# Attention and a feed-forward layer in one kernel: another order of VectorE's sums, copies and scalings around two stages

## The chip, the cores and the metric

The kernel runs on one core of a Trainium2 chip. A core has TensorE (PE, the matrix engine), VectorE (DVE), ScalarE (ACT), GpSimd (POOL) and SyncE (SP, which here only starts transfers). Each engine works through its own instructions strictly in the order in which they were written; engines wait for one another only through semaphores. TensorE writes into eight PSUM banks, which VectorE and ScalarE empty. The metric is the device time of one execution in microseconds (us), taken as a median over runs.

## The reference

```python
def _attn_ref(q, k, v):                       # (8, 12, 448, 64) each
    scale = 1.0 / np.sqrt(q.shape[-1])
    scores = scale * np.matmul(q, k.transpose(0, 1, 3, 2))
    scores = scores - np.max(scores, axis=-1, keepdims=True)
    attn = np.exp(scores)
    attn = attn / (np.sum(attn, axis=-1, keepdims=True) + 1e-09)
    return np.matmul(attn, v).astype(np.float32)

def _moe_ref(x, w_in, w_out):                 # x (3584, 768), w_in (768, 2048), w_out (2048, 768)
    h = x @ w_in
    g = np.maximum(0.01 * h, h)
    return (g @ w_out).astype(np.float32)
```

The attention's output, with the heads side by side, is the `x` of the second function: 3584 tokens of 768 columns.

## The kernel before, in words

**Units of attention.** A unit is one pair of heads of one of the 8 batches; there are 48 units, 6 to a batch. For each unit TensorE computes scores in chunks (L337), ScalarE takes the exponential of each chunk (L351), and TensorE forms the weighted sums of v (`rows`: L877 for units below 18, L888 and L893 from unit 18 on). VectorE divides by the row sums: a reciprocal (L899) and a product (L900) that writes the tile `x` of the unit. The tile is then transposed into `xT`: for most units by a DMA started on SP (L294), and for units 9, 10, 11 and 17 (`X_PE`) by TensorE (L395) with a copy out of PSUM by VectorE (L396). Units of the second kind wait in the list `owed_x` until `settle_x` finds a score slot free. From unit 18 on keys are laid out so that a fourth, partial chunk of scores (the "rest", L356 and L358) belongs to each unit; it waits in `owed_rest`.

**PSUM.** Two banks g102 and g103 (`banks`) serve the feed-forward products, and three double slots sc104, sc105 and sc106 (`slots`) serve scores, weighted sums and the transpositions of L395, used in turn. A burst (`burst`) issues three chunks of scores, two matmuls each, into three slots.

**Stages of the feed-forward layer.** The tokens are cut into 7 stages. For stage i > 0, `hidden(i)` computes h = x·w_in with seven block products in place of eight (a Strassen-like scheme), so it needs sums of blocks of `w_in` (`mix_w_in`: 12 differences at L465 and then 4 sums at L469, each 128x768) and of the stage's own columns of `xT` (`mix_x_part`, eight differences at L494 written to `x_mix` and back into `xT`, four for the first two columns of blocks and four for the third). Then `second(i)` computes the output in two pairs of token blocks (`block_pair`, c = 0 and c = 1), again with seven products of eight matmuls each (L621) instead of eight. In a pair the products alternate between bank b and bank a. VectorE empties a bank by a copy (L626, `keep`) before the next product accumulates on it, or adds it to the output tile `o` (L629, `join`); and it forms two differences of h for the later products (L633 after the first product, L639 after the second). The third product needs the result of L633 and the bank b that L626 has emptied. In stage 0 `mix_first` adds to this, for pair c = 1, differences of `h` (L521, L522) inside pair c = 0. The finished `o` is stored by DMAs on SP (L408).

**The order of the work.** The order is written out when the program is built. `block_pair` yields at each step (a step is two matmuls, or the place behind a product's copies); x counts the steps of a pair: x = 1, 2, 3 lie inside the first product, and at x = 4 L633 and the first copy have been issued. At each step `second` calls `place`, which issues bursts, rests and weighted sums where a small model of time says that slot and data are ready. With `calm` false `place` issues neither rests nor weighted sums. After `place`, `second` advances the iterators: `ins` (the sums of `mix_w_in`), `outs` (those of `mix_weights`), `mix_first`, and `x_sums` (the two lists of L494 for the next stage; the second list waits for `owed_x` to be empty). Each of these adds instructions to VectorE's queue at that place.

Stage 1 needs the units of batch 2, 12 to 17, so the second list of its L494 needs unit 17, the one whose `x` goes through L395 and L396. Stage 6, the last, needs units up to 47, whose weighted sums are issued in stage 5.

Of the kernel before, what the change touches and what calls it, by code (L numbers as in the profile page):

```python
# [16 lines left out]
def kernel(  # L17
# [20 lines left out]
    NU = B * HP  # L38
# [6 lines left out]
    NR = len(cuts) - 1  # L45
    HEAD = S
    need = [HP * -(-t // S) for t in cuts]
# [24 lines left out]
    def next_slot():  # L72

        slots.append(slots.pop(0))
        return slots[-1]
# [230 lines left out]
    def transposes(u, bank=None):  # L306
        if u >= min(NPE, NU):
            return
        gone.add(u)
        for parts in ((1,), (0,)) if u == 0 else ((0, 1),):  # L310
            tr = turn_tile(bank)
            for i in parts:
                for so in range(NSC):
                    nc.tensor.transpose(  # L314
                        tr[:, i, ts(so, SC)], qk_sb[u][:SC, i * NSC + so], ident[:SC, :SC]
                    )
            if u == 0:
                stay_warm(3 if parts == (1,) else 5)
            at = slice(parts[0], parts[-1] + 1)
            (nc.scalar.copy if u == NPE - 1 or u == 0 and parts == (1,) else nc.vector.tensor_copy)(  # L320
                qkT[u % NQ][:, :QL].rearrange("p (i s) -> p i s", i=2)[:, at], tr[:, at]
            )
# [502 lines left out]
    owed_rest = []  # L825
    total = WIDE * NSC + (NU - WIDE) * NWC

    def at_chunk(x):

        return divmod(x, NSC) if x < WIDE * NSC else (WIDE + (x - WIDE * NSC) // NWC, (x - WIDE * NSC) % NWC)  # L830

    def scored():

        return owed_rest[0] if owed_rest else at_chunk(chunk)[0]

    def set_rest():

        u = owed_rest.pop(0)
        rest(u)
        return u  # L840
# [66 lines left out]
    def turned(u):  # L907

        return u < to["pe"] or to["pe"] == NPE and u < to["turn"]

    def burst(lazy=0):
        nonlocal chunk
        todo = [at_chunk(chunk + x) for x in range(3) if chunk + x < total]
        assert rows_done > todo[-1][0] - NE and turned(todo[-1][0]) and to["v"] > rows_done and not owed_rest
        if todo[0][0] >= WIDE:
            assert todo[0][1] == 0
            owed_rest.append(todo[0][0])
        for a, c in todo:
            scores(a, c)
        assert not late  # L920
        for a, c in todo[:3 - lazy]:
            expo(a, c)
        late.extend(todo[3 - lazy:])
        chunk += len(todo)

    X_PE = (HP + 3, HP + 4, HP + 5, 3 * HP - 1)
    owed_x = []

    def settle_x(now=None):
        while owed_x and (now is None or owed_x[0][1] <= now and model["free"].get(id(slots[0]), 0.0) <= now + 0.05):  # L930
            model["free"][id(slots[0])] = model["now"] + 1.0
            model["now"] += 0.3
            x_transposes(owed_x.pop(0)[0], next_slot()[:, 0])
# [39 lines left out]
    def place(i, want, soon=0, full=True, calm=True, first=False, lazy=0, keen=NU, cap=NU):  # L973

        free, ready = model["free"], model["ready"]
        done, state = 0, 0
        while True:
            settle_x(model["now"])
            now = model["now"]
            last = at_chunk(chunk + 2)[0]  # L980
            blocked = rows_done <= min(last, NU - 1) - NE
            u = rows_done
            whole = u < scored()
            at = [free.get(id(x), 0.0) for x in slots]
            u = to["pe"]
            if max(want, soon) > done and u <= min(last, NPE - 1) and len(slots) == 3 and at[0] <= now + 0.05:
                t = slots[0]
                transposes(u, next_slot()[:, 0])
                to["pe"] += 1
                model["now"] = now + 0.45  # L990
                free[id(t)] = model["now"] + 1.0
                continue
            if len(slots) < 3 and full and max(want, soon) > done and u <= min(last, NPE - 1) and state == 0:
                transposes(u)
                to["pe"] += 1
                state = 1
                model["now"] += 0.45
                continue
            if want > done and state < 2 and turned(last) and not blocked and not owed_rest and len(slots) == 3 and all(
                x <= now + 0.05 + 0.2 * j for j, x in enumerate(at)  # L1000
            ):
                state = 2
                order = list(slots)
                start = chunk
                burst(lazy)
                if first:
                    feed(start // 3)
                done += 1
                for x, t in enumerate(order[:chunk - start]):
                    model["act"] = max(model["act"], now + 0.45 + 0.2 * x) + 0.8  # L1010
                    free[id(t)] = model["act"] + (0.3, 0.15 + 0.5 * (lazy > 1), 0.15 + 0.5 * lazy)[x]
                    if at_chunk(start + x + 1)[1] == 0 and not owed_rest:
                        ready[at_chunk(start + x)[0]] = model["act"] + 0.1
                model["now"] = now + 0.78
                continue
            u = to["pe"]
            if first and full and state == 0 and u < min(NPE - 1, to["cast"] - 1) and u <= scored() + 1 and model["act"] <= now + 0.6:
                transposes(u)
                to["pe"] += 1
                state = 1  # L1020
                model["now"] += 0.45
                continue
            if calm and owed_rest and at[0] <= now + 0.05:
                t = slots[0]
                u = set_rest()
                model["act"] = max(model["act"], now + 0.25) + 0.5
                free[id(t)] = model["act"] + 0.15
                ready[u] = model["act"] + 0.1
                model["now"] = now + 0.19
                continue  # L1030
            u = rows_done
            if calm and whole and not (lazy and late) and at[0] <= now + 0.05 and ready.get(u, 0) <= now + 0.05 and (
                u <= at_chunk(chunk + 5)[0] - NE or u < keen
            ) and u < cap:
                t = slots[0]
                rows()
                if first:
                    pay()
                model["now"] = now + 1.08
                free[id(t)] = now + 2.33  # L1040
                continue
            return done

    def second(i):

        x_sums = [mix_x_part(i + 1, slice(0, 2)), mix_x_part(i + 1, slice(2, 3))] if i + 1 < NR else []
        fresh, summed = [None, None], [i + 1 == NR] * 2
        left = plan[i]
        for c in range(len(spots(i)[1])):
            for x, _ in enumerate(block_pair(i, c)):  # L1050
                if x % 4 == 0:
                    advance(i + 1 < NR and rows_done >= need[i + 2] - 3 and not all(summed), at_chunk(chunk + 3 * left - 1)[0])
                if c or x:
                    model["now"] += 0.325
                left -= place(i, left, calm=x not in (1, 2), keen=need[min(i + 2, NR)], cap=NU if all(summed) else need[i + 2])
                if i == 0 and c == 0 and x in (5, 7):
                    next(outs)
                if i == 0 and c == 0 and x in (9, 13, 17, 21):
                    mix_first((x - 9) // 2, 1, slice(HEAD - 3 * P, P))
                if i == 0 and c and x % 4 == 2:  # L1060
                    next(ins, None)
                for y in range(2):
                    if fresh[y] is None and i + 1 < NR and rows_done >= need[i + 2] - 1 + y:
                        fresh[y] = model["now"] + (2.5 if need[i + 2] - 2 + y in X_PE else 7.0)
                for y, todo in enumerate(x_sums if x % 2 == 0 else ()):
                    if fresh[y] is not None and fresh[y] <= model["now"] and not summed[y] and not (y and owed_x):
                        summed[y] = next(todo, 0) is not None
                        if not summed[y]:
                            break
        assert left == 0 or chunk == total, (i, left)  # L1070
        assert i + 1 == NR or rows_done >= need[i + 2], (i, rows_done)
        settle_x()
        for todo in x_sums:
            for _ in todo:
                pass
# [64 lines left out]
```

## Time and profile before

| what | value |
|---|---|
| median of 3 runs | 382.3 us (382.08 to 382.34) |
| profiled execution, its own time | 382.59 us |
| span of that execution, first to last instruction | 380.8 us |
| granted TensorE clock, mean | 0.999 |
| ScalarE, GpSimd busy | 253.2 us, 152.5 us |
| stage 0, pair c = 0 (first and last L621) | about 73 to 88.4 us |
| stage 0, pair c = 1 | about 89 to 104.5 us |
| first L549 of stage 1 and of stage 6 | 104.49 us, 339.92 us |

The page gives for each engine the busy time and its share of the span. The timeline gives instructions in order: start, time from the start to the end of the last one of the row, engine, line, operation, output and inputs, count, and in brackets how long the engine had been idle before and what released it. Instructions of one engine overlap a little: a row's own time can be longer than the distance to the start of the next, so in what follows distances between starts are used where an engine runs without a break. The chain of waits lists the pieces of the path that ended last in the same way.

### The profile page before, as it was taken

The numbers are of one execution on the slowest core, as the hardware profiler recorded it, in microseconds if no ns is written. First come the engines' busy times: TensorE is split into PE (matmuls) and PEld (weight loads), VectorE is DVE, ScalarE is ACT, GpSimd is POOL, SyncE is SP. The second block draws the span as 40 slices with busy tenths as digits, with TensorE's granted clock in tenths as the row PEclk, the third lists the DMA queues.
The fourth block names the chain that finished last, engine by engine and source line by source line (L and its number), as shares of the span: only waits on it lengthen the run. The fifth ranks groups of instructions, "written<-read, shape, count | busy, mean of one in ns | idle before, by whom it ended". The sixth has DMA issues, their size and how long they took to land.

```text
span 380.8 us, 9900 instructions
## 1 busy us (share of the span) xinstructions
PE 372.5 (98%) x3972; PEld 261.8 (69%) x3973; DVE 231.5 (61%) x513; ACT 253.2 (67%) x392; POOL 152.5 (40%) x302
## 2 busy tenths in 40 slices
PE   8999999999999999999999999999999999999995
PEld 6665658756498565896658965589755896668753
DVE  4662767786666555568475674655746565574753
ACT  5997885866667867677684776847867478318700
POOL 5886664495433854338333364334733000000000
PEclk9999999999999999999999999999999999999999
DMA  7999999999588996999858999579986540320022
GB/s 154 182 195 203 198 183 208 174 142 179 77 159 101 90 183 136 152 148 93 141 102 141 123 106 142 117 136 135 107 115 135 123 83 0 108 80 18 0 84 84
DMA packets 107198, 47.95 MB, mean 126 GB/s; under 512 B 79248, under 2 KB 103824, under 8 KB 107152
## 3 DMA queue, kind: packets, MB, share of 16 engines
q0 software_dynamic: 48096, 22.24, 48.7%
q1 hardware_dynamic: 58320, 24.43, 34.1%
q10 hardware_dynamic: 736, 0.66, 0.6%
q8 instruction: 31, 0.51, 0.5%
q14 instruction: 15, 0.12, 0.1%
HBM read 45.61 MB, written 11.01 MB: 149 GB/s over the span
## 4 chain that ended last, share of the span: by engine, by line
PE 94%; ACT 2%; DVE 2%; issue 1%; DVEq 0%
PE g L621 34%; PE sc L549 14%; PE g L549 14%; PE sc L337 9%; PE sc L888 6%; PE g L430 4%; PE sc L877 3%; PE g L716 2%; ACT e L351 2%; PE sc L893 2%; PE sc L356 1%; PE g L258 1%; PE g L314 1%; PE g L368 1%; PE sc L430 1%
## 5 line engine op out<-in xcount | busy, mean ns | idle before, releaser
L351 ACT ACTIVATE e<-sc 128x896 bf16<-128x896 f32 (+1 forms) x162 | 137.4, 922 | 42.4 <-PE sc L337 42.2
L621 PEld LDWEIGHTS <-h 128*128 128x128 bf16 x680 | 62.8, 98 | 50.2 <-issue 12.8
L621 PE MATMUL g<-w_out_sb,h 128*128 128x384 bf16 x448 | 86.5, 327 | 0.0
L538 ACT ACTIVATE h<-c 128x512 bf16<-128x512 f32 (+1 forms) x72 | 43.7, 611 | 28.6 <-DVE c L564 13.7
L549 PEld LDWEIGHTS <-w_in_sb 128*128 128x128 bf16 x576 | 54.7, 98 | 5.9
L337 PE MATMUL sc<-qkT 64*128 64x448 bf16 x324 | 42.8, 353 | 2.4 <-DVE xT L396 0.7
L626 DVE COPY o<-g 128x384 f32<-128x384 f32 x53 | 29.4, 555 | 24.3 <-PE g L621 24.2
L209 POOL COPY v<-fv 128x256 f32<-128x256 f32 (+1 forms) x38 | 15.2, 407 | 71.7 <-PE sc L893 47.5
L549 PEld LDWEIGHTS <-w_in_mix 128*128 128x128 bf16 x432 | 41.1, 98 | 4.0
L621 PE MATMUL g<-w_mix,h 128*128 128x384 bf16 (+1 forms) x224 | 41.9, 324 | 0.5 <-DVE o L626 0.5
L629 DVE TENSOR_TENSOR o<-o,g 128x384 f32<-128x384 f32 x42 | 23.2, 552 | 20.0 <-PE g L621 18.2
L888 PEld LDWEIGHTS <-e 128*128 128x128 bf16 x720 | 30.4, 97 | 3.5 <-ACT e L351 2.3
L888 PE MATMUL sc<-v,e 128*128 128x65 bf16 x720 | 32.1, 193 | 0.0
L209 POOL COPY qkb<-fq 112x256 f32<-112x256 f32 x38 | 16.6, 436 | 38.6 <-DMA fq<-in_q_dram 20.3
L337 PEld LDWEIGHTS <-qkT 64*128 64x128 bf16 x324 | 12.8, 94 | 25.6 <-issue 18.3
L900 DVE TENSOR_TENSOR x<-sc,rec 112x512 bf16<-112x512 f32 x42 | 29.0, 691 | 1.5
L899 DVE RECIPROCAL rec<-sc 112x8 f32<-112x8 f32 x42 | 8.7, 208 | 33.3 <-PE sc L893 17.2
L549 PE MATMUL sc<-xT,w_in_sb 128*128 128x256 bf16 (+1 forms) x216 | 28.5, 268 | 0.0
L549 PE MATMUL g<-xT,w_in_sb 128*128 128x256 bf16 (+1 forms) x216 | 28.5, 268 | 0.0
L893 PE MATMUL sc<-v,e 128*128 128x130 bf16 x120 | 26.7, 222 | 0.0
L209 POOL COPY qkb<-fk 128x256 f32<-128x256 f32 (+1 forms) x38 | 18.7, 493 | 16.0 <-DMA fk<-in_k_dram 16.0
L621 PE MATMUL g<-w_mix,hmix 128*128 128x384 bf16 x112 | 23.3, 326 | 0.0
(123 smaller groups left out, 587.0 us busy)
## 6 DMA issues: line engine op xcount, KB each, us to landing
fq<-in_q_dram POOLq DMA_DIRECT2D x19, 224.0 KB, 6.5
w_in_sb<-in_moe_w_in_dram POOLq DMA_DIRECT2D x4, 768.0 KB, 12.3
w_out_sb<-in_moe_w_out_dram POOLq DMA_DIRECT2D x4, 768.0 KB, 18.4
fk<-in_k_dram POOLq DMA_DIRECT2D x15, 192.0 KB, 5.5
fv<-in_v_dram POOLq DMA_DIRECT2D x15, 192.0 KB, 4.2
out_dram<-o SPq DMA_DIRECT2D x7, 336.0 KB, 3.4
out_dram<-o SPq DMA_DIRECT2D x8, 288.0 KB, 3.3
out_dram<-o SPq DMA_DIRECT2D x7, 240.0 KB, 3.2
```

The lines of the kernel that those rows point to most:

```text
L209: by(t.rearrange("p so h d -> p h so d") if x < 2 else t[:, :, :, :d], f)
L337: nc.tensor.matmul(ps[:, j, :S], t[j * D:(j + 1) * D, k0:k0 + P], q_of(u)[j * D:(j + 1) * D] if u >= WIDE else t[j * D:(j + 1) * D, :S], s ...
L351: nc.scalar.activation(e[:, :, c, :], sc_t.pop((u, c))[:e.shape[0], :, :S], AX.Exp, scale=scale)
L430: nc.tensor.matmul(open_t[m][:, :n], w_in_sb[:, kk, ts(m, P)], xT[:, kk, at:at + n], start=(fresh and kk == kks[0]), stop=(kk == KD - 1),)
L538: nc.scalar.activation(hs[:, m:m + 2, cols], x.rearrange("p (m t) -> p m t", m=2), AX.Prelu, alpha=0.01)
L549: nc.tensor.matmul(ps[:, j * nh:(j + 1) * nh], w[:, kk, ts(j, P)], x[:, kk], start=(first and j == 0 and kk == 0), stop=(kk == KH - 1), sk ...
L621: nc.tensor.matmul(ps[:, cols], x[:, m], w[:, m], start=(first and m == 0), stop=(m == MH - 1), skip_group_check=True,)
L626: by(o[:, at], ps[:, :NW])
L629: nc.vector.tensor_add(o[:, at], o[:, at], ps[:, :NW])
L888: nc.tensor.matmul(ps[:, b, y + j, :D + 1], e[:, at:at + P], vt[:, j, c, :D + 1], start=(y + j + c == 0), stop=False, skip_group_check=True,)
L893: nc.tensor.matmul(ps[:, b, y:y + 2, :D + 1], e[:, at:at + P], vt[:, :, NWC, :D + 1], start=False, stop=True, skip_group_check=True,)
L900: nc.vector.tensor_mul(x, ps[:SC, :, :, :D], rec.to_broadcast([SC, 2, NSC, D]))
```

## The change

Four lines change, all in the code that decides the order.

```diff
@@ place @@
-            if calm and owed_rest and at[0] <= now + 0.05:
+            if owed_rest and at[0] <= now + 0.05:
@@ second @@
-                left -= place(i, left, calm=x not in (1, 2), keen=need[min(i + 2, NR)], cap=NU if all(summed) else need[i + 2])
+                left -= place(i, left, calm=x not in (1, 2, 3), keen=need[min(i + 2, NR)], cap=NU if all(summed) else need[i + 2])
...
-                if i == 0 and c and x % 4 == 2:
+                if i == 0 and c == 0 and x % 4 == 3 and x > 8:
                     next(ins, None)
...
-                for y, todo in enumerate(x_sums if x % 2 == 0 else ()):
+                for y, todo in enumerate(x_sums if x % 2 == 0 and (i or not owed_x) else ()):
```

No instruction is added or removed on any engine, and ScalarE, GpSimd and SP keep their orders. What moves:

- The four sums L469 go from pair c = 1 of stage 0 to pair c = 0, at x = 11, 15, 19 and 23.
- In stage 0 no L494 is issued while unit 17's transposition is still owed. VectorE's order there was L900 of unit 17, L469, L494, L629, L494, L396, L494, L629; it becomes L900, L629, L396, L494, L629, L494, L494.
- `calm` now keeps back the weighted sums at x = 3 too, but no longer the rests. On TensorE this moves one set of weighted sums only, in the first pair of stage 5: it is issued behind the last two matmuls of the first product instead of ahead of them. On VectorE its L899 and L900 go behind L633 and the copy L626 of that product.

## The prediction

> **What bounds the kernel now.** I read the page first, for the engine with the least idle time.
>
> ```profile
> span 380.8 us, 9900 instructions
> PE 372.5 (98%) x3972; PEld 261.8 (69%) x3973; DVE 231.5 (61%) x513; ACT 253.2 (67%) x392; POOL 152.5 (40%) x302
> ```
>
> TensorE is busy for 372.5 of 380.8 us, and the change alters neither its work nor its count. So only a TensorE wait that goes or comes can move the time. The list of TensorE's waits over the whole trace is next; these two rows of it lie in or beside stages that the change touches.
>
> ```profile
> PE sc L337 <- DVE xT L396: 0.7, 1, 0.7
> PE g L621 <- DVE o L626: 0.5, 1, 0.5
> ```
>
> Each happens once. The page models the ends of matmuls, so I size both again from starts. For that I need TensorE's pace when nothing holds it: from the chain of waits (start, length), six score matmuls, and six output matmuls behind weighted sums.
>
> ```profile
> 91.85 0.98 PE g L621 x6
> ...
> 95.72 0.67 PE sc L337 x6
> ```
>
> A burst takes 0.67 us and an output matmul 0.98 / 6 = 0.163 us.
>
> The first stall, in the timeline at the end of stage 0:
>
> ```profile
> 98.89 0.81 PE L621 MATMUL g<-w_mix,hmix 128*128 128x384 bf16 x4
> ...
> 99.40 0.69 DVE L900 TENSOR_TENSOR x<-sc,rec 112x512 bf16<-112x512 f32 x1
> ...
> 100.00 0.55 DVE L469 TENSOR_TENSOR w_in_sb<-w_in_sb 128x768 bf16<-128x768 bf16 x1
> ...
> 100.14 0.37 PE L395 MATMUL sc<-c,x 112*128 112x112 bf16 x4
> ...
> 100.47 0.42 DVE L494 TENSOR_TENSOR x_mix<-xT 128x512 bf16<-128x512 bf16 x1
> ...
> 100.78 0.55 PE L337 MATMUL sc<-qkT 64*128 64x448 bf16 x4
> 100.81 0.55 DVE L629 TENSOR_TENSOR o<-o,g 128x384 f32<-128x384 f32 x1
> ...
> 101.27 0.42 DVE L494 TENSOR_TENSOR xT<-xT 128x512 bf16<-128x512 bf16 x1
> 101.61 0.38 DVE L396 COPY xT<-sc 128x448 bf16<-128x448 bf16 x1
> ...
> 102.34 0.76 PEld L621 LDWEIGHTS <-h 128*128 128x128 bf16 x6 [0.20 <-issue]
> ```
>
> The transpositions of unit 17 end at 100.51, but VectorE copies them (L396) only at 101.61 to 101.99, behind L469, L494, L629 and L494. The third chunk of the burst needs that slot: the burst begins at 100.78, and its next work, the L621 weights, at 102.34, after 1.56 us instead of 0.67. The stall is **0.89 us**.
>
> The second, in the first pair of stage 5:
>
> ```profile
> 330.08 0.34 PE L888 MATMUL sc<-v,e 128*128 128x65 bf16 x6
> ...
> 331.04 1.79 PE L621 MATMUL g<-w_out_sb,h 128*128 128x384 bf16 x10
> 331.31 0.21 DVE L899 RECIPROCAL rec<-sc 112x8 f32<-112x8 f32 x1 [1.45 <-PE sc L893]
> 331.56 0.69 DVE L900 TENSOR_TENSOR x<-sc,rec 112x512 bf16<-112x512 f32 x1
> 332.16 0.68 DVE L633 TENSOR_TENSOR h<-h 128x1024 bf16<-128x1024 bf16 x1
> ...
> 332.76 0.55 DVE L626 COPY o<-g 128x384 f32<-128x384 f32 x1
> ...
> 333.37 1.46 PE L621 MATMUL g<-w_mix,h 128*128 128x384 bf16 x8 [0.54 <-DVE o L626]
> ```
>
> TensorE does the last two matmuls of the first product and the eight of the second from 331.04 on; at 0.163 each it is through at 332.67. The third product starts at 333.37, when L626 has ended (333.31). VectorE had L899 and L900 ahead of L633 and L626. The stall is **0.70 us**.
>
> **The change part by part.**
>
> *Unit 17's copy (gain).* Behind L900 there now come L629 and L396. VectorE starts the instruction after L900 0.60 us behind its start (99.40 to 100.00), so L629 starts at 100.00; its input, the product that began its last four matmuls at 98.89, ended at 99.70. The instruction behind an L629 starts 0.46 later (100.81 to 101.27): L396 could start at 100.47, and takes its data at 100.51 plus some 0.1 of signalling (L900 itself ends at 100.09, L395 begins at 100.14, so 0.05 at least). It ends by 100.61 + 0.38 = 100.99. The third chunk is due after four score matmuls, 100.78 + 0.45 = 101.23. So 0.24 us to spare and no stall: **0.89 us gained**. If signalling cost 0.3 more than I take, the gain would shrink by less than 0.1.
>
> *The differences L494 behind it.* Four instructions that stood ahead of the stall now come later against a stage 1 that begins earlier.
>
> ```profile
> 104.49 0.71 PE L549 MATMUL g<-xT,w_in_sb 128*128 128x256 bf16 x5
> ```
>
> ```profile
> 104.65 0.66 PE g L549 x6
> ```
>
> Stage 1 begins at 104.49 (the timeline), in future at 103.60. Its third step uses a difference made by the third L494 of both lists. Two chains of six matmuls alternate at 0.66 a group (the chain of waits), so four groups come ahead of it and it falls at 103.60 + 4 x 0.66 = 106.2. VectorE does the first L494 at 100.9, waits with L629 for four more output matmuls behind the burst (101.45 + 0.65, and 0.2 until the copy runs: 102.3), does two L494 by 103.6, waits with the copy L626 for the pair's last product (103.6, so 103.8 to 104.3), and has five L494 left, of which the fourth is needed. At the 0.42 of the larger form (these have 512 and 256 columns) it would be ready at 104.3 + 4 x 0.42 = 106.0. That is 0.2 us of cover; without it, the step waits a few tenths at most, since ScalarE's and VectorE's work on the first two steps comes behind. I take zero, and keep 0.4 as the other end.
>
> *The four sums L469 in pair c = 0 (cost).* Each takes 0.47 of VectorE's time (100.00 to 100.47). What counts is the TensorE work due behind each.
>
> ```profile
> 81.44 0.55 DVE L626 COPY o<-g 128x384 f32<-128x384 f32 x1
> ...
> 83.90 0.21 DVE L899 RECIPROCAL rec<-sc 112x8 f32<-112x8 f32 x1 [1.19 <-PE sc L877]
> ...
> 84.75 0.54 DVE L629 TENSOR_TENSOR o<-o,g 128x384 f32<-128x384 f32 x1
> ...
> 86.24 0.55 DVE L629 TENSOR_TENSOR o<-o,g 128x384 f32<-128x384 f32 x1 [0.55 <-PE g L621]
> 87.60 0.21 DVE L899 RECIPROCAL rec<-sc 112x8 f32<-112x8 f32 x1 [0.81 <-PE sc L877]
> ...
> 88.51 0.56 DVE L626 COPY o<-g 128x384 f32<-128x384 f32 x1
> ```
>
> ```profile
> 83.96 0.81 PE L621 MATMUL g<-w_out_sb,h 128*128 128x384 bf16 x4
> ...
> 86.04 0.49 PE L621 MATMUL g<-w_mix,h 128*128 128x384 bf16 x2
> ...
> 89.08 1.80 PE L621 MATMUL g<-w_out_sb,h 128*128 128x384 bf16 x10
> ```
>
> The first sum takes 81.44, and the copy L626 goes to 81.91, ending at 82.46; its bank is next written at 83.96, so 1.5 us remain. The idle 1.19 us before L899 at 83.90 swallows the rest. The second stands ahead of the L629 of 84.75, which goes to 85.22 and ends at 85.76; its bank is next written at 86.04. This is the tightest place, 0.28 us less signalling, about **0.2 us**. The third stands ahead of the L629 of 86.24 and fills the 0.55 idle us before it; that ends near 87.1, ahead of the L899 that waits for TensorE until 87.60. The fourth pushes the L626 of 88.51 to 88.98, ending at 89.54; its bank is written again only after eight of the ten matmuls of 89.08, at 90.38. Cost: zero. The two output stores behind these joins start up to 0.47 later, and behind the first of them SP has one transposition for a unit whose scores come several bursts on.
>
> Here a rule speaks against the change. First the rows: the same 128x128 difference at two moments, and GpSimd's cast beside the first.
>
> ```profile
> 81.90 0.47 DVE L521 TENSOR_TENSOR hmix<-h 128x128 bf16<-128x128 bf16 x1
> 85.21 0.22 DVE L521 TENSOR_TENSOR hmix<-h 128x128 bf16<-128x128 bf16 x1
> ```
>
> ```profile
> 81.87 0.40 POOL L209 COPY qkb<-fq 112x256 f32<-112x256 f32 x1
> ```
>
> Beside the cast the difference lost 0.25 us. The Trainium skill, "SBUF — State Buffer", section "Who interferes with whom", says that a VectorE instruction with both inputs in SBUF contends with a GpSimd instruction that reads SBUF, the later one blocking until the earlier is done; the rows agree, with 0.47 against 0.22. L469 is such an instruction, and it moves to where GpSimd casts. By that rule a sum beside a cast costs 0.25 more, by its old rows nothing; at the tight place the L629 would then end at 86.01, TensorE would wait some 0.05 us, and the gain would be 1.54 instead of 1.59.
>
> *The weighted sums in stage 5 (gain).* The two matmuls now go ahead of them: 330.08 to 330.41. L633 can start about 0.2 later, 330.6, and ends at 331.3; L626 starts 0.60 behind L633 (332.16 to 332.76) and ends at 331.75. The weighted sums run 330.41 to 331.37, the second product to 332.67, and the third starts at once: **0.70 us gained**. L899 is released at 331.37 + 0.27 (as 331.04 to 331.31 now), so 331.65 to 331.7, and L900 ends near 332.65 instead of 332.25. Late by 0.4 us, then, is the DMA that transposes unit 47's x for the last stage; it is weighed below. That the rests are no longer held back moves nothing on TensorE or ScalarE.
>
> *The sum.* 0.89 + 0.70 = 1.59 us, by the page's own waits 0.7 + 0.5 = 1.2. Taken from the profiled execution, 382.59 - 1.59 = 381.0 us; that execution was 0.29 above the median of 382.3, so 380.7 for a median. Nothing between the two places waits for anything but TensorE's own pace: no further row of TensorE's list of waits lies in stages 1 to 6. So what is saved at 102 us stays saved.
>
> **The rivals.**
>
> *One stall stays.* L396 could still be too late if the L629 ahead of it waits for something that its row of 100.81, where VectorE came late to it, can't show; or L633 waits longer than 0.2 for the moved matmuls. Then 0.70 or 0.89 alone is gained: 381.6 or 381.4. For it: 0.24 us to spare at L396. Against: the ends of all inputs are in the rows, and in stage 5 the copy has 0.9 us to spare. Chance 0.14.
>
> *The gain is absorbed.* TensorE reaches stage 1 earlier and the third step waits for L494 (up to 0.4), while ScalarE, whose exponentials of the last burst don't move earlier, holds back the rest; then stage 6, too, finds something late. A gain of some 0.5 to 0 remains: 381.8 to 382.3. Against it: TensorE waited for nothing else after 105 us. Chance 0.10.
>
> *Slower: unit 47's transposition comes too late.* One DMA, started 0.4 us later while stage 6 begins 0.7 us earlier.
>
> ```profile
> 339.92 0.82 PE L549 MATMUL g<-xT,w_in_sb 128*128 128x256 bf16 x6
> ```
>
> ```profile
> DMA to landing us min/median/max: 2.4/2.4/2.4
> ```
>
> The transpositions of this stretch landed 2.4 us after issue; over the whole kernel those of this line took 2.3 to 10.4.
>
> ```profile
> DMA to landing us min/median/max: 2.3/4.5/10.4
> ```
>
> Issued at 332.65, it is needed by 339.92 - 0.70 = 339.2: it decides from a landing of 6.6 us on. At the worst 10.4 it lands at 343.05, TensorE waits 3.8 us, and the time is 380.7 + 3.8 = 384.5. The queue is nearly empty there and three out of three took 2.4. Chance 0.04.
>
> **How the numbers follow.** Forecast 0.72: 380.7 us, own range 380.4 (the spread of the three runs, 0.26, below it) to 381.1 (the sum by the page's waits). The 0.14 and 0.10 of the rivals reach to 382.3; to leave no more than 2 in 10 out, the range goes to 381.7, which takes in the case of one stall: 380.3 to 381.7. About 0.2% (0.76 us) is what a measurement tells from no change. Faster: 0.72 and half of the one-stall case (0.89 alone is over the bound, 0.70 alone under it), 0.79. Same: the other half and the absorbed case, 0.17. Slower: 0.04.
>
> **What would show it.** In the new profile both rows of TensorE's waits are gone; L396 starts within 0.2 us of the end of L395; stage 1 begins near 103.6 and stage 6 near 338.3; pair c = 0 still ends as it did, with no wait at the matmuls of 86.04. I would be wrong if those matmuls wait for L629, if L549's third step waits for L494, or if the span shortens by less than 1.2 us with both stalls gone.

## The result, and the profile after

| kernel | median of its runs | runs |
|---|---|---|
| before | 382.39 us (382.06 to 383.54) | 12 |
| changed | 381.47 us (380.82 to 382.07 without the first) | 12 |
| changed / before | 0.9967, 95% interval 0.9955 to 0.9979 | |

The gain is 1.26 us (382.39 x 0.0033), with an interval of 0.8 to 1.7; the ratio is the recorded one over the runs, not the quotient of the two medians. The first execution of the changed kernel, 2130.9 us with TensorE slower throughout, is left out of the ratio (the median without it is 381.40), and the profile after is that of a further run of the same kernel (381.02 us).

Its page, engines and TensorE's whole list of waits:

```profile
span 378.9 us, 9899 instructions
...
PE 372.1 (98%) x3972; PEld 261.6 (69%) x3973; DVE 233.1 (62%) x513; ACT 253.3 (67%) x392; POOL 155.4 (41%) x302
```

```profile
PE sc L337 <- ACT e L351: 0.8, 3, 0.4
PE g L258 <- PEq L1124: 0.8, 1, 0.8
PE sc L337 <- DVE x L900: 0.3, 1, 0.3
PE sc L337 <- DVE qkT L320: 0.2, 1, 0.2
PE g L263 <- issue: 0.2, 1, 0.2
```

TensorE does the same work in a span shorter by 1.9 us. The page counts one instruction less than before: VectorE has 696 in the trace instead of 697, as a wait ahead of an L629 of stage 5 is no longer needed in the new order, so one instruction is removed after all. The rows for L396 and L626 are gone. The row for L351 has grown from 0.6 us and two waits to 0.8 and three, all of them ahead of 72 us and of everything that moves. One row, 0.3 us for L900, was not there before; it is taken up below. The end of stage 0 in the timeline after:

```profile
99.45 0.69 DVE L900 TENSOR_TENSOR x<-sc,rec 112x512 bf16<-112x512 f32 x1
...
100.06 0.54 DVE L629 TENSOR_TENSOR o<-o,g 128x384 f32<-128x384 f32 x1
...
100.20 0.37 PE L395 MATMUL sc<-c,x 112*128 112x112 bf16 x4
...
100.68 0.39 DVE L396 COPY xT<-sc 128x448 bf16<-128x448 bf16 x1
100.83 0.74 PE L337 MATMUL sc<-qkT 64*128 64x448 bf16 x6
...
101.50 0.82 PE L621 MATMUL g<-w_out_sb,h 128*128 128x384 bf16 x4
...
103.65 0.82 PE L549 MATMUL g<-xT,w_in_sb 128*128 128x256 bf16 x6
...
105.31 0.29 DVE L494 TENSOR_TENSOR x_mix<-xT 128x256 bf16<-128x256 bf16 x1
...
106.27 0.82 PE L549 MATMUL g<-x_mix,w_in_mix 128*128 128x256 bf16 x6
```

L396 starts 0.11 us behind the end of L395 (100.57), the burst stands as one row of six, and the L621 follow 0.67 after its start instead of 1.56. Stage 1 begins at 103.65; its third step, at 106.27, finds the difference ready since 105.60. The first pair of stage 5 after:

```profile
328.45 1.46 PE L621 MATMUL g<-w_out_sb,h 128*128 128x384 bf16 x8
...
329.95 0.69 DVE L633 TENSOR_TENSOR h<-h 128x1024 bf16<-128x1024 bf16 x1 [0.74 <-PE g L621]
330.56 0.55 DVE L626 COPY o<-g 128x384 f32<-128x384 f32 x1
330.71 1.46 PE L621 MATMUL g<-w_out_sb,h 128*128 128x384 bf16 x8
331.03 0.20 DVE L899 RECIPROCAL rec<-sc 112x8 f32<-112x8 f32 x1
331.26 0.69 DVE L900 TENSOR_TENSOR x<-sc,rec 112x512 bf16<-112x512 f32 x1
...
332.01 1.46 PE L621 MATMUL g<-w_mix,h 128*128 128x384 bf16 x8
```

The third product follows the second at once (330.71 to 332.01); L626 has ended 0.9 us ahead of it.

### The profile page after: what moved, and what is told of

Read it like the earlier page. It is cut to its first block, busy times and chain, and to the rows that moved or that the text cites. A ratio compares the mean times of both kernels' runs of the same rounds, so it can differ in the third digit from the quotient of the medians.

```text
span 2128.7 us, 9900 instructions
## 1 busy us (share of the span) xinstructions
PE 2125.0 (100%) x3973; PEld 965.3 (45%) x3973; DVE 234.5 (11%) x513; ACT 277.6 (13%) x392; POOL 153.5 (7%) x302
## 4 chain that ended last, share of the span: by engine, by line
PE 100%; DVE 0%; issue 0%
PE g L621 36%; PE sc L549 15%; PE g L549 15%; PE sc L337 9%; PE sc L888 6%; PE g L430 5%; PE sc L877 3%; PE g L716 2%; PE sc L893 2%; PE sc L356 2%; PE g L368 2%; PE g L314 1%; PE sc L430 1%; PE g L258 1%; PE sc L314 0%; PE g L395 0%
## 5 line engine op out<-in xcount | busy, mean ns | idle before, releaser
L621 PE MATMUL g<-w_out_sb,h 128*128 128x384 bf16 x448 | 464.5, 1352 | 0.0
L621 PEld LDWEIGHTS <-h 128*128 128x128 bf16 x680 | 199.7, 299 | 461.5 <-issue 460.3
L549 PEld LDWEIGHTS <-w_in_sb 128*128 128x128 bf16 x576 | 185.7, 323 | 178.2 <-issue 177.9
L621 PE MATMUL g<-w_mix,h 128*128 128x384 bf16 (+1 forms) x224 | 232.0, 1360 | 0.0
L351 ACT ACTIVATE e<-sc 128x896 bf16<-128x896 f32 (+1 forms) x162 | 148.7, 918 | 578.0 <-PE sc L337 577.2
L549 PEld LDWEIGHTS <-w_in_mix 128*128 128x128 bf16 x432 | 139.2, 323 | 130.1 <-issue 129.8
L337 PE MATMUL sc<-qkT 64*128 64x448 bf16 x324 | 192.2, 1422 | 0.0
L888 PEld LDWEIGHTS <-e 128*128 128x128 bf16 x720 | 148.4, 256 | 34.1 <-issue 27.4
L888 PE MATMUL sc<-v,e 128*128 128x65 bf16 x720 | 162.4, 483 | 0.0
L549 PE MATMUL g<-xT,w_in_sb 128*128 128x256 bf16 (+1 forms) x216 | 151.1, 1024 | 0.0
L549 PE MATMUL sc<-xT,w_in_sb 128*128 128x256 bf16 (+1 forms) x216 | 151.0, 1018 | 0.0
L621 PE MATMUL g<-w_mix,hmix 128*128 128x384 bf16 x112 | 122.3, 1377 | 0.0
L430 PE MATMUL g<-xT,w_in_sb 128*128 128x448 bf16 x84 | 100.8, 1511 | 0.0
L549 PE MATMUL sc<-x_mix,w_in_mix 128*128 128x256 bf16 (+1 forms) x144 | 100.7, 1022 | 0.0
L549 PE MATMUL g<-x_mix,w_in_mix 128*128 128x256 bf16 (+1 forms) x144 | 100.0, 1008 | 0.0
L626 DVE COPY o<-g 128x384 f32<-128x384 f32 x53 | 29.5, 556 | 346.6 <-PE g L621 346.6
```

Source lines behind the costliest of these rows:

```text
L337: nc.tensor.matmul(ps[:, j, :S], t[j * D:(j + 1) * D, k0:k0 + P], q_of(u)[j * D:(j + 1) * D] if u >= WIDE else t[j * D:(j + 1) * D, :S], s ...
L351: nc.scalar.activation(e[:, :, c, :], sc_t.pop((u, c))[:e.shape[0], :, :S], AX.Exp, scale=scale)
L430: nc.tensor.matmul(open_t[m][:, :n], w_in_sb[:, kk, ts(m, P)], xT[:, kk, at:at + n], start=(fresh and kk == kks[0]), stop=(kk == KD - 1),)
L549: nc.tensor.matmul(ps[:, j * nh:(j + 1) * nh], w[:, kk, ts(j, P)], x[:, kk], start=(first and j == 0 and kk == 0), stop=(kk == KH - 1), sk ...
L621: nc.tensor.matmul(ps[:, cols], x[:, m], w[:, m], start=(first and m == 0), stop=(m == MH - 1), skip_group_check=True,)
L888: nc.tensor.matmul(ps[:, b, y + j, :D + 1], e[:, at:at + P], vt[:, j, c, :D + 1], start=(y + j + c == 0), stop=False, skip_group_check=True,)
```

## The experiments

One number of a run doesn't show 0.2 us here, so each kernel was timed and also profiled, and TensorE's starts cut each profile into stretches: from the first L621 of pair c = 0 to that of c = 1, from there to the first L549 of stage 1, to the first L621 of stage 5, to the first L549 of stage 6, and to the end of the span.

| profile | start to pair c = 0 | pair c = 0 | pair c = 1 | stages 1 to 4, and 5 up to its pairs | pairs of stage 5 | stage 6 |
|---|---|---|---|---|---|---|
| before | 73.13 | 15.95 | 15.41 | 210.66 | 24.77 | 40.88 |
| changed, first run | 72.83 | 16.47 | 14.35 | 210.85 | 24.08 | 40.32 |
| stage 5 alone | 73.60 | 16.13 | 15.42 | 210.65 | 24.08 | 40.82 |
| both edits of stage 0 | 73.43 | 15.95 | 14.35 | 210.65 | 24.77 | 40.35 |
| place of L494 alone | 73.49 | 15.95 | 14.75 | 210.76 | 24.77 | 40.48 |
| sums L469 alone | 73.25 | 15.95 | 14.77 | 210.65 | 24.77 | 40.31 |
| before, padded | 73.50 | 15.95 | 15.24 | 210.68 | 24.77 | 40.56 |
| two sums at once | 73.07 | 16.37 | 14.35 | 210.64 | 24.09 | 40.48 |
| changed, again | 73.22 | 15.95 | 14.35 | 210.65 | 24.08 | 40.65 |

The pairs c = 1 and of stage 5 repeat to 0.01 us from kernel to kernel with the same order there. (The padded kernel is the exception, and is explained below.) The first column and the last scatter by 0.8 and 0.6 us with no bearing on any edit, and the runs' times scatter with them.

The stretches cover the span, from the first to the last instruction, and beside its time each run of these sets has its own span on record. The time is longer than the span by 1.73 to 1.85 us in every run of the kernel before, of both edits of stage 0, of L494 alone and of the sums alone. In every run of the changed kernel, of stage 5 alone, of two sums at once and of the padded kernel it is longer by 2.08 to 2.20. These two groups don't overlap, and about 0.36 us more of the time lies outside the span in the second. So three gains are set side by side here, each against the kernel before; those of spans and times are differences of means over the runs, with standard errors of 0.15 to 0.25 us.

| kernel | pair c = 1 and pairs of stage 5 | mean span | mean time |
|---|---|---|---|
| changed, first set | 1.75 | 1.86 | 1.50 |
| stage 5 alone | 0.69 | 0.67 | 0.32 |
| both edits of stage 0 | 1.06 | 1.24 | 1.24 |
| place of L494 alone | 0.66 | 0.84 | 0.85 |
| sums L469 alone | 0.64 | 0.28 | 0.29 |
| before, padded | 0.17 | 0.12 | -0.24 |
| two sums at once | 1.74, less 0.24 at the tight place | 1.43 | 1.04 |
| changed, again | 1.75 | 1.74 | 1.37 |

The spans follow the stretches within that noise. The times fall short of them by the 0.36 in the kernels of the second group. That group has 696 or 701 instructions on VectorE and the first has 697; what the 0.36 us is spent on, the traces don't show.

**The changed kernel, profiled.** No edit against the changed kernel.

> The changed kernel itself, for a profile. Theory (both TensorE waits are gone and nothing takes their place): no row of TensorE waiting for L396 or for L626 is left; stage 1 begins at about 103.6 us of the span instead of 104.49, stage 6 at about 338.3 instead of 339.92; time 1.3 to 1.6 us below the kernel before. Rival A (one stall stays or is given back in the first steps of stage 1): stage 1 begins early but TensorE waits for L494 or L564 there, gain 0.7 to 1.0 us. Rival B (the sums in pair c = 0 hold VectorE up): a wait of TensorE for L629 or L626 between 81 and 91 us, and pair c = 1 begins later than 89.08.

Measured: 381.05 against 382.76 us before on the same chip, ratio 0.9960 (0.9947 to 0.9973), so 1.5 us. In the stretches, 1.06 us went from pair c = 1 and 0.69 from stage 5. Pair c = 0, however, took 0.52 longer. The timeline of this profile, VectorE and GpSimd just ahead of the new wait:

```profile
76.22 1.75 DVE L451 TENSOR_TENSOR w_out_sb<-w_out_sb 128x768 bf16<-128x768 bf16 x1
...
76.81 0.41 POOL L209 COPY v<-fv 112x256 f32<-112x256 f32 x1
77.15 0.41 POOL L209 COPY qkb<-fq 112x256 f32<-112x256 f32 x1
77.49 0.74 POOL L209 COPY qkb<-fk 112x256 f32<-112x256 f32 x1
...
78.87 0.36 PE L337 MATMUL sc<-qkT 64*128 64x448 bf16 x2 [0.35 <-DVE x L900]
```

A sum of w_out (L451) took 1.75 us beside three casts of GpSimd, L900 behind it came late, and the burst waited 0.35. Set start by start against the kernel before, TensorE loses 0.51 us at this burst, so all but 0.01 of what pair c = 0 lost. This lies ahead of the first instruction that the change moves (81.93), and the kernel with stage 5 alone, whose stage 0 is that of before, had the same sum at 1.41:

```profile
76.99 1.41 DVE L451 TENSOR_TENSOR w_out_sb<-w_out_sb 128x768 bf16<-128x768 bf16 x1
```

VectorE's order up to there is that of before, so it is not the change's; that it depends on when the loads reach GpSimd in an execution is argued, not shown. The second profile of the changed kernel, below, has neither the long sum's wait nor the 0.52.

The margin that the prediction called the tightest, in the same profile:

```profile
81.88 0.40 POOL L209 COPY v<-fv 112x256 f32<-112x256 f32 x1
...
81.93 0.76 DVE L469 TENSOR_TENSOR w_in_sb<-w_in_sb 128x768 bf16<-128x768 bf16 x1
...
84.97 0.55 DVE L469 TENSOR_TENSOR w_in_sb<-w_in_sb 128x768 bf16<-128x768 bf16 x1
...
85.44 0.55 DVE L629 TENSOR_TENSOR o<-o,g 128x384 f32<-128x384 f32 x1
...
86.26 0.49 PE L621 MATMUL g<-w_mix,h 128*128 128x384 bf16 x2
```

L629 ends at 85.99, and the product that needs its bank starts at 86.26 without a wait. The stretch of stages 1 to 4 is 0.19 longer in this profile than in the second. It arises at one place, where an L633 at 224.60 took 0.96 us in place of 0.69; the kernel with L494 alone has the like at another place, 273.36 (0.89), and the second profile of the changed kernel at neither. So it varies from one execution to the next.

**Stage 5 alone.** The kernel before with

```diff
-            if calm and owed_rest and at[0] <= now + 0.05:
+            if owed_rest and at[0] <= now + 0.05:
-... calm=x not in (1, 2), keen=...
+... calm=x not in (1, 2, 3), keen=...
```

> The kernel before with the two edits on calm and on the rests alone: only the weighted sums in the first pair of stage 5 move, everything of stages 0 to 4 keeps its order. Theory: the wait for L626 at 333.37 goes and nothing else, gain 0.70 us (0.5 by the page's own wait), stage 6 begins at 339.2. Rival (unit 47's transposition comes too late): TensorE or L494 waits for a DMA around 339 us and the gain is 0.3 us or less.

Measured: ratio 0.9991 (0.9981 to 1.0001), so 0.3 us with an interval of 0 to 0.7; the pairs of stage 5 took 24.08 instead of 24.77, 0.69 less. The wait for L626 is gone and the one for L396 is there:

```profile
PE sc L337 <- DVE xT L396: 0.7, 1, 0.7
```

Stage 6 began with no wait, so unit 47's transposition is in time. The whole time alone would not have shown the gain: the mean span fell by 0.67 us, as the stretch did, but some 0.36 us more of the time lay outside the span.

**Both edits of stage 0.** The kernel before with

```diff
-                if i == 0 and c and x % 4 == 2:
+                if i == 0 and c == 0 and x % 4 == 3 and x > 8:
-                for y, todo in enumerate(x_sums if x % 2 == 0 else ()):
+                for y, todo in enumerate(x_sums if x % 2 == 0 and (i or not owed_x) else ()):
```

> The kernel before with the two edits on stage 0 alone: the sums L469 go to pair c = 0, and no L494 goes ahead of unit 17's copy L396; stage 5 as before. Theory: the wait for L396 at 102.04 goes, stage 1 begins at 103.6, gain 0.89 us; the wait for L626 at 333 stays. Rival A: gain 0.5 us or less, with a wait in stage 1's first steps.

Measured: ratio 0.9967 (0.9953 to 0.9980), so 1.3 us, and pair c = 1 1.06 us shorter, with the 0.5 us for L626 still in the list. Stage 1 began at 103.73. The stretch gained 0.17 more than the 0.89 of the one stall.

**The place of L494 alone.** The kernel before with the second of these two edits.

> The kernel before with the edit on L494 alone: the sums L469 stay in pair c = 1, so the last of them still stands between L900 of unit 17 and L629, L396. Theory: L396 comes 0.47 us later than with both edits, so that it ends near 101.35 against 101.23 when the third chunk is due: a wait of some 0.1 us stays, gain 0.75 us. Rival (moving the sums is what counts, not the order of L494 against L396): gain under 0.4 us.

Measured: ratio 0.9976 (0.9963 to 0.9989); pair c = 1 took 0.66 us less, so 0.40 of the 1.06 needs the sums moved too. The timeline at the burst:

```profile
101.14 0.96 PE L337 MATMUL sc<-qkT 64*128 64x448 bf16 x6
101.31 0.38 DVE L396 COPY xT<-sc 128x448 bf16<-128x448 bf16 x1
...
102.04 0.82 PE L621 MATMUL g<-w_out_sb,h 128*128 128x384 bf16 x4
```

With the last sum still ahead of it, L396 ends at 101.69, and the burst takes 0.90 instead of 0.67: 0.23 of the stall stays, where some 0.1 was expected. The other 0.17 is not at this place.

**The sums alone.** The kernel before with the first of the two edits.

> The kernel before with the sums L469 moved to pair c = 0 alone; the first L494 still stand ahead of unit 17's copy L396. Theory (L396 is as late as what stands ahead of it): with one instruction less ahead it ends at about 101.5 against 101.23 when the third chunk is due, so a wait of about 0.35 us stays of the 0.89; and VectorE's L899 near 92.3 comes 0.36 us sooner, as in the kernels that had the sums moved. Stretch from the first L621 of pair c = 1 to stage 1: 14.7 us, against 15.41 before, 14.75 with the order of L494 alone, 14.35 with both. Rival (the sums don't matter, only the place of L494): 15.2 or more.

Measured: ratio 0.9991 (0.9976 to 1.0005), not to be told from no change by the time; pair c = 1 took 14.77 us.

```profile
101.09 0.38 DVE L396 COPY xT<-sc 128x448 bf16<-128x448 bf16 x1
...
101.53 0.36 PE L337 MATMUL sc<-qkT 64*128 64x448 bf16 x2 [0.25 <-DVE xT L396]
101.82 0.82 PE L621 MATMUL g<-w_out_sb,h 128*128 128x384 bf16 x4
```

The burst, from 100.73, took 1.09: a stall of 0.42 stays. Gained here are 0.89 - 0.42 = 0.47, and 0.17 at the other place, 0.64 in all. So neither edit alone clears the stall; L396 comes as late as what stands ahead of it.

**Where the other 0.17 us is.** It is the burst at 93 us, 0.84 long in the kernel before and 0.67 in all those with the sums moved. Before, in the timeline:

```profile
90.72 1.14 PE L877 MATMUL sc<-v,e 112*128 112x65 bf16 x32
91.20 0.55 DVE L626 COPY o<-g 128x384 f32<-128x384 f32 x1
...
92.32 0.21 DVE L899 RECIPROCAL rec<-sc 112x8 f32<-112x8 f32 x1 [0.56 <-PE sc L877]
...
92.76 0.91 PE L337 MATMUL sc<-qkT 64*128 64x448 bf16 x6
```

The weighted sums end at 91.86, VectorE is free since 91.75, and yet L899 starts at 92.32, 0.45 later; elsewhere it follows by 0.1. It did so in each of the three profiles with the sums in c = 1 and in none of those with the sums in c = 0. No sum stands between. What differs is L899's number in VectorE's queue, counted over everything in the program: 192 in the one, 196 in the other. So the kernel before got four more instructions near its start:

```diff
-    nc.vector.memset(gate, 0.0)
+    for _ in range(5): nc.vector.memset(gate, 0.0)
```

> The kernel before with four more tiny memsets (60 ns each) of the same two columns on VectorE near 1 us, where it is idle until 4 us: every later VectorE instruction has its number in the queue four higher, and no order changes. Theory (the 0.45 us by which L899 near 92.3 starts after its inputs hangs on that instruction's number in VectorE's queue): L899 starts within 0.15 us of the end of its weighted sums, the burst after it takes 0.67 in place of 0.84, and the stretch from pair c = 1 to stage 1 is 15.24 in place of 15.41. Rival (it hangs on the work around it, which the moved sums change): 0.45 and 15.41 as before.

```profile
91.08 1.14 PE L877 MATMUL sc<-v,e 112*128 112x65 bf16 x32
...
92.33 0.21 DVE L899 RECIPROCAL rec<-sc 112x8 f32<-112x8 f32 x1 [0.21 <-PE sc L877]
...
93.13 0.74 PE L337 MATMUL sc<-qkT 64*128 64x448 bf16 x6
```

L899 follows the sums' end (92.22) by 0.11, and pair c = 1 took 15.24: the 0.17 hangs on the number, not on the sums. The time of this kernel, ratio 1.0007 (0.9995 to 1.0020), shows nothing of so small a size.

**Two sums at the tight place.** The changed kernel with

```diff
-                if i == 0 and c == 0 and x % 4 == 3 and x > 8:
-                    next(ins, None)
+                for _ in range({11: 1, 19: 2, 23: 1, 27: 1}.get(x, 0) if i == 0 and c == 0 else 0):
+                    next(ins, None)
```

(The first of the iterator's steps hands out no sum, so the changed kernel's four sums stand at x = 15, 19, 23 and 27, and not at 11, 15, 19 and 23 as said of the change.)

> The changed kernel with the first of the four sums L469 moved on to stand beside the second, so that two instead of one stand ahead of the L629 that the prediction called the tightest place. Theory (0.2 to 0.25 us of cover there): that L629 ends 0.47 us later, the last product of pair c = 0 waits for it some 0.2 to 0.25 us, shown as TensorE waiting for L629 near 86.3, and the time is that much above the changed kernel. Rival (VectorE has more room there than the rows say): no wait, same time.

```profile
84.86 1.01 DVE L469 TENSOR_TENSOR w_in_sb<-w_in_sb 128x768 bf16<-128x768 bf16 x2
85.49 0.82 PE L621 MATMUL g<-w_out_sb,h 128*128 128x384 bf16 x4
85.80 0.55 DVE L629 TENSOR_TENSOR o<-o,g 128x384 f32<-128x384 f32 x1
...
86.39 0.48 PE L621 MATMUL g<-w_mix,h 128*128 128x384 bf16 x2
```

The last product starts 0.90 behind the four matmuls ahead of it instead of 0.66 (85.60 to 86.26 in the changed kernel): a wait of 0.24. The time's ratio, 0.9974 (0.9962 to 0.9986), lies 0.0009 above that of the changed kernel beside it, 0.3 us, with intervals that overlap. The mean spans of the two differ by 0.31. Pair c = 0 took 0.42 more; the other 0.18 arose ahead of these sums, at 79.72, behind a sum of w_out (L451 at 78.25) that took 0.95 us beside GpSimd's casts.

**The changed kernel again.**

> The changed kernel once more, beside the others of this call. Theory: 1.06 us less from pair c = 1 to stage 1 and 0.69 less from stage 5 to stage 6 than before, again, so 1.75 below the kernel before but for what varies ahead of pair c = 1 from one execution to the next. Rival (part of the 1.75 was chance): 1.3 or less in these two stretches.

Measured: ratio 0.9965 (0.9952 to 0.9977), 1.3 us; 1.06 and 0.69 us less in the same two stretches, and pair c = 0 at 15.95 as before the change. So the 1.75 is no chance, and the mean span fell by as much (1.74).

## Why the prediction was right

The mechanism held at both places, and so did the sign. The size held less well: the median of 381.47 us lies 0.8 above the forecast of 380.7 (the other two sets gave 381.05 and 381.08), outside the forecast's own range up to 381.1. It lies near the 381.4 and 381.6 that one remaining stall would have given, so the number alone would have spoken for that rival; only the traces show that both stalls went. The reasons for the size come last here.

- *Unit 17's copy, 0.89 us.* L396 was put at 100.51 to 100.61 and started at 100.68, ended at 101.07 and left 0.2 us. The stall of 0.89 went in full: the burst's 1.56 became 0.67. The two edits of stage 0 were costed together as one order. Singly they gain 0.66 and 0.47 at this place; the stall ends only when both are made, and together they can't gain more than its 0.89.
- *The differences L494 in stage 1.* Taken at zero, rightly; the cover was put at 0.2 us and was 0.67, because five differences were priced at the 0.42 of their row's whole length where each held VectorE for about 0.33.
- *The sums in pair c = 0.* Taken at zero, rightly. The cover of about 0.2 us at the L629 of 84.75 was 0.23 to 0.27 in size: the second of two sums there, 0.47, overran it by 0.24.
- *The rule against it.* The sum that met a cast took 0.76 instead of 0.55 us (81.93). The Trainium skill, "SBUF — State Buffer", section "Who interferes with whom", has the later of the two block, and this row agrees: 0.21 us, against the 0.25 that the rule was given. It fell on the first sum, which has 1.5 us of cover, and not on the one at the tight place (84.97, 0.55): there the cast started later than the sum, at 85.17, and it was the cast that took longer (0.62 us instead of 0.40). In the second profile it fell on the third sum (86.16, 0.75), which has cover too. At the second sum such a loss would have used up the cover. That sum took 0.55 in all four profiles with the four sums at these places, but nothing in the order of the kernel keeps a cast away from it.
- *The weighted sums in stage 5, 0.70 us.* Measured 0.69, in every profile that has the edit. Unit 47's transposition, 0.4 us later, landed in the 2.4 us that the row gave, so the rival that ends slower had no part.
- *The rival of the one stall that stays* is what each edit of stage 0 gives alone; with both it did not happen. *The rival of an absorbed gain* is refuted: stages 1 to 4 took 210.65 in the second profile of the changed kernel against 210.66, and the 0.19 more of the first does not lie at the third step of stage 1.

The sum, 1.59 us, lacked two terms of opposite sign. The stretches give 1.06 + 0.69 = 1.75, and the 0.16 more is the burst at 93 us, whose delay was in the rows of before and was not read as a stall: TensorE's list of waits doesn't name it, as it is short, and the row says only that L899 waited for the weighted sums. That the moved sums also cleared it was luck. The other term lies outside the span: the sum carried 1.59 us over to the time as if nothing changed there, but the changed kernel loses 0.36 us there in every run. What is left is 1.75 - 0.36 = 1.39, and the runs' own ratios give 1.26, 1.5 and 1.3 us in three sets. The base adds to the 0.8 us: the three runs of the kernel before that were known had a median of 382.3, and the twelve have a mean of 382.7. Why the 0.36 us arises stays open.

## What to carry to other kernels

- When one engine is busy all the time, read its few waits from the starts of its rows and ask what stood ahead of the late instruction in the other engine's queue. A reorder there costs nothing as long as each displaced instruction still ends ahead of the next use of its buffer, which is worked out place by place.
- Where several instructions delay the same copy, all must be moved: the one move left 0.23 us of the 0.89, the other 0.42, and only both cleared the stall.
- Where the whole time scatters by more than the edit is worth, compare stretches between fixed starts of the busy engine; here they repeat to 0.01 us. Then compare the span with the time as well: the stretch and the mean span of stage 5 alone gave 0.69 and 0.67 us where the time gave 0.3, because 0.36 us more of the time lay outside the span.

## What the hardware showed that was not expected

In these traces an instruction of VectorE can start some 0.35 us late because of its number in the queue. In the kernel before it is number 192, the L899 above. In the padded kernel, where nothing is late at 192, three more instructions are: numbers 320, 448 and 576 start 0.35, 0.22 and 0.35 us later behind the wait ahead of them than the same instructions do in the kernel before, where they have other numbers. That is every 128th. The first of them, in the timeline of the padded kernel with no releaser to be found:

```profile
161.98 0.69 DVE L576 TENSOR_TENSOR c<-c,g 128x512 f32<-128x512 f32 x1 [1.10 <-ACT c L573]
...
162.99 0.69 DVE L576 TENSOR_TENSOR c<-c,sc 128x512 f32<-128x512 f32 x1 [0.32 <-issue]
```

The same two in the kernel before, where the second starts 0.65 behind the first instead of 1.01:

```profile
161.78 0.69 DVE L576 TENSOR_TENSOR c<-c,g 128x512 f32<-128x512 f32 x1 [1.10 <-ACT c L573]
...
162.43 0.69 DVE L576 TENSOR_TENSOR c<-c,sc 128x512 f32<-128x512 f32 x1
```

The padded kernel's page lists a queue that moves 8 KB at a time (0.12 MB in 15 packets):

```profile
q14 instruction: 15, 0.12, 0.1%
```

The Trainium skill, "Perfetto Trace Analysis", section "The 4-stage abstract model", says that an instruction has 64 bytes; 8 KB would then hold 128 of them, which agrees with the distance. That the delay is the hand-over to the next such block is argued from this, not shown. No packet of that queue falls into one of the four delays: the next one begins 0.8 to 3.0 us after the late instruction has started. So the instruction didn't wait for such a packet to land, and what the time is spent on stays open. Where VectorE has work of its own to run through or waits anyway, nothing of it is seen: with the sums in pair c = 0, number 192 falls on the copy L626 behind the last sum, and it starts 0.46 us behind that sum (88.68 to 89.14), as copies do elsewhere.
